# A larger booked cost for the matmuls in a kernel's own list scheduler

## The chip, the core and the metric

The kernel runs on one core of a Trainium2 chip. The metric is the device time of one execution in microseconds (us). The core's engines are called by the profile's names: PE (TensorE, matmuls), DVE (VectorE), ACT (ScalarE), POOL (GpSimd) and SP (which here only issues DMAs). Each engine runs its own instructions strictly in the order in which they were issued, and waits on semaphores for the others.

## What is computed

Causal attention with a cumulative decay (4 batches of 8 heads, 576 positions, head size 64), then a gated feed-forward, then a low-rank mix over the positions with a second feed-forward:

```python
attn = softmax(q @ k.T / 8 + min(-(cum_i - cum_j), 0), causal) @ v   # x: [4, 576, 512]
h    = relu(x @ w_in)                                 # 512 -> 1024
x    = (h * sigmoid(conv3(h))) @ w_out                # 1024 -> 512
u    = x + (x^T @ U @ V)^T                            # rank 32 over the positions
out  = u + relu(u @ w_ch1) @ w_ch2                    # 512 -> 2048 -> 512
```

Everything is float32. The kernel gets this precision by splitting each operand into a high and a low part and using three matmuls where one would do (high by high, high by low, low by high).

## The kernel before

**Stages.** The span falls into stages that overlap: the attention heads and the first feed-forward together (to about 413 us; `m1_in` makes `h`, `m1_out` makes `y`), the mix (`mix_a`, `mix_t`, `mix_b`; T, x and u), then `m2_in` (428 to 629 us) and `m2_out` (629 to 826 us).

`m2_in(f, g)` (L1139 and on) computes one block of the second feed-forward's first product with Strassen's scheme in Winograd's form: seven products, named in program order A11, S2, A12, S3, S1, A22, S4, for each of 8 blocks f of the weights and 4 blocks g of the tokens. One product is six matmuls of 288 columns into one PSUM bank, so a group is 42 matmuls. A bank becomes free when its readers are done. A11, A12 and S4 are read by a copy on ACT (`p1`, `p2`). S2, S3, S1 and A22 are read by additions on DVE at L1169 (`s6`, `s7`, `s5`, `c2`). So `s6_1_1` is the addition that frees the bank of product `ma1_1_S2`.

The operands of `m2_in` are made while it runs. Weights come packed and are decoded by one instruction at L504 and two at L514 on DVE (`wf_w2a3_1` is half 1 of block 3), then added and subtracted at L1115 (`S12`, `S34`). The token blocks T1 to T4 are made by subtractions at L1052. In this text "filler" means these instructions of DVE: nothing on PE waits for them at once, whereas the additions of L1169 hold banks.

**The scheduler.** No instruction is issued where it is written. Each piece of work is recorded as `plan.op(engine, cost, ...)`, with a cost in nanoseconds. `Plan.order()` (L182 on) then simulates the engines with these costs: it takes the engine that is free first, gives it the ready piece that stands first in program order, and books its cost. The order in which the simulated engines took the pieces is the order in which they are issued. So a cost never appears as a wait on the chip, but it decides what stands in front of what, on all engines.

The eight PSUM banks are handed out in the same simulation. Among the banks that are already free at the simulated time, the one freed last is taken:

```python
ready = [i for i in idle if idle[i] <= t]
if ready and used[b.cls] < CAPS[b.cls]:
    o, slot = top[2], min(ready, key=lambda i: -idle[i])
```

So the plan hands a bank on at once if it believes that its reader has just finished. On the chip, the semaphore decides.

**Costs.** `mm(n)` (L347) is the cost of one matmul of n columns. It is used, times the count, for the scores of heads 8 and up (`2*mm`, L675), `m1_in` (`3*mm(290)`, L868), `m1_out` (`3*mm(288)`, L910), `mix_b` (`mm(288)`, L973), `m2_in` (`6*mm(288)`, L1153) and `m2_out` (`3*mm(512)` and `3*mm(256)`, L1252). DVE is booked by L328, which has two fixed parts, 70 ns early and 155 ns late in the program, and 1.042 ns per column (0.52 for the copies and the shift of L504). Scores of heads 0 to 7, transposes and the products with v have costs of their own.

Of the kernel before, what the change touches and what calls it, by code (L numbers as in the profile page):

```python
# [308 lines left out]
def tile_attention_moe_mixer(  # L309
# [35 lines left out]
        return plan.op("PE", ns, fn, r, w)  # L345

    def mm(n, m=128):  # L347
        return max(n / 2.4 + 3, m / 1.2)


    def hi_act(out, src, r, w, n):
# [318 lines left out]
    def products(h, ps, rows, q0, k0, w):  # L670
        d = st[h]

        def mms():
            for c, t in enumerate(d["qk"]):
                nc.tensor.matmul(  # L675
                    ps[:rows, :w],
                    lhsT=t[:, 0, q0 : q0 + rows],
                    rhs=t[:, 1, k0 : k0 + w],
                    start=c == 0,
                    stop=c == len(d["qk"]) - 1,  # L680
                )

        pe(16 + 1.88 * w if h in FS else 2 * mm(w, rows), mms, d["qk"], [ps])
# [173 lines left out]
    def m1_in(b, hf, f):  # L857
        ps = bank("h", f"h{b}_{hf}_{f}")
        c0 = hf * HS
        for kt in range(KT):  # L860
            th, tl = xs[b, kt]

            def mms(kt=kt, th=th, tl=tl):
                a, l = th[:, c0 : c0 + W], tl[:, c0 : c0 + W]
                wh = w1h[f, 0][:, kt * 128 : kt * 128 + 128]
                wl = w1l[f, 0][:, kt * 128 : kt * 128 + 128]
                for n, (ww, xx) in enumerate(((wh, a), (wh, l), (wl, a))):
                    nc.tensor.matmul(  # L868
                        ps[:, :W], lhsT=ww, rhs=xx, start=kt + n == 0, stop=kt == KT - 1 and n == 2
                    )  # L870

            pe(3 * mm(W), mms, [w1h[f, 0], w1l[f, 0], th, tl], [ps])
# [26 lines left out]
    def m1_out(b, hf, dt):  # L899
        if hf == 0:  # L900
            x2[b, dt] = ring(mx, "x2", RINGS["x2"], [128, S], F32, f"x2_{b}_{dt}")
        ps = bank("y", f"y{b}_{hf}_{dt}")
        for f in range(NF1):
            gh, gl = gs[b, hf, f]

            def mms(f=f, gh=gh, gl=gl):
                c0 = dt * 128
                wh, wl = w1h[f, 512][:, c0 : c0 + 128], w1l[f, 512][:, c0 : c0 + 128]
                for n, (ww, xx) in enumerate(((wh, gh), (wh, gl), (wl, gh))):
                    nc.tensor.matmul(  # L910
                        ps[:, :HS], lhsT=ww, rhs=xx(), start=f + n == 0, stop=f == NF1 - 1 and n == 2
                    )

            pe(3 * mm(HS), mms, [w1h[f, 512], w1l[f, 512], gh, gl], [ps])
        o = x2[b, dt]
        act(HS, lambda: nc.scalar.mul(o[:, hf * HS : hf * HS + HS], ps[:, :HS], 2.0**-9), [ps], [(o, hf)])
# [654 lines left out]
```

## Time and profile before

| | |
|---|---|
| time, median of 3 runs | 833.66 us (832.91 to 836.38) |
| the profiled execution's own time | 831.95 us |
| its span, first to last instruction | 830.2 us |
| PE busy | 791.6 us (95%) |
| DVE, ACT, POOL busy | 538.2, 454.3, 360.0 us |
| mean granted clock of PE | 0.996 |

PE is busy for 95% of the span and so idle for 38.6 us. About half of the idle time lies in the first 100 us. The trace has three things to look at: how PE's idle time is spread over the stages, what ended each idle stretch, and what the engine that ended it was doing before. "Idle" behind an instruction is the time for which its engine stood still just before it.

### The profile page before, as it was taken

How to read it: one execution, taken by the hardware profiler on the slowest of the kernel's cores; microseconds unless marked ns; L12 is line 12 of the kernel's file. 1: busy time of each engine (PE TensorE's matmuls, PEld its weight loads, DVE VectorE, ACT ScalarE, POOL GpSimd, SP SyncE). 2: the span in 40 equal slices, each digit the busy share in tenths (PEclk: the TensorE clock that was granted, in tenths of full speed). 3: DMA queues.
4: the chain of work that ended last, by engine and by line, in shares of the span. 5: the costliest groups of instructions: out<-in, count | busy, mean ns of one | idle time of the engine just before them, and what ended most of it. 6: DMA issues, size and time to landing. Idle time of an engine off the chain costs nothing. (4 is left out here: it accounts for less than half of the span.)

```text
span 830.2 us, 15394 instructions
## 1 busy us (share of the span) xinstructions
PE 791.6 (95%) x5300; PEld 709.2 (85%) x5300; DVE 538.2 (65%) x1182; ACT 454.3 (55%) x1144; POOL 360.0 (43%) x441
## 2 busy tenths in 40 slices
PE   4898899999999999999989999999999999999998
PEld 2566788999899999999988898999998888888888
DVE  6887797636855378556998989777688632323232
ACT  4897898858878488767656334324344322222212
POOL 4786684634537234383284776455564200000000
PEclk9999999999999999999999999999999999999999
DMA  7657755734466247030235335446378563636443
GB/s 212 184 170 192 167 154 149 167 97 107 142 144 156 60 111 208 5 109 1 85 109 181 126 133 191 162 150 191 123 220 301 154 193 100 189 103 184 114 127 98
DMA packets 66310, 119.70 MB, mean 144 GB/s; under 512 B 9396, under 2 KB 34868, under 8 KB 66232
## 3 DMA queue, kind: packets, MB, share of 16 engines
q1 hardware_dynamic: 66160, 118.70, 49.7%
q8 instruction: 42, 0.69, 0.4%
q14 instruction: 36, 0.29, 0.1%
q10 hardware_dynamic: 72, 0.01, 0.0%
HBM read 68.81 MB, written 28.90 MB: 118 GB/s over the span
## 5 line engine op out<-in xcount | busy, mean ns | idle before, releaser
L1252 PE MATMUL my<-mh,w 128*128 128x512 f32 (+1 forms) x560 | 158.8, 368 | 0.0
L1153 PE MATMUL ma_S<-u,W 128*128 128x288 f32 x768 | 120.5, 298 | 5.0 <-DVE s L1169 5.0
L1233 DVE SCALAR_TENSOR_TENSOR ml<-ml,mh 128x512 fp32r<-128x512 f32 (+1 forms) x80 | 53.1, 672 | 105.2 <-ACT mh L1230 105.0
L1230 ACT ACTIVATE mh<-ml 128x512 fp32r<-128x512 f32 (+1 forms) x80 | 46.9, 589 | 128.3 <-DMA ml<-ch_d 76.9
L1252 PEld LDWEIGHTS my<-mh,w 128*128 128x128 f32 x560 | 101.7, 189 | 17.5
L910 PE MATMUL y<-gh,w1o 128*128 128x288 f32 x512 | 114.2, 301 | 1.1 <-POOL w1o L364 1.0
L1153 PEld LDWEIGHTS ma_S<-u,W 128*128 128x128 f32 x768 | 108.3, 189 | 7.2 <-DVE s L1169 7.1
L664 POOL TENSOR_SCALAR P<-P,sm 128x128 f32<-128x128 f32 (+3 forms) x128 | 77.1, 618 | 80.3 <-DVE sm L727 63.2
L1252 PE MATMUL my<-ml,w 128*128 128x512 f32 (+1 forms) x280 | 103.0, 368 | 0.0
L1153 PE MATMUL ma_A<-u,W 128*128 128x288 f32 x576 | 92.5, 295 | 0.9 <-ACT p L1165 0.9
L636 DVE CUSTOM_DVE_ANT_0 sc<-sc,mask 128x128 f32<-128x128 f32 (+2 forms) x144 | 68.6, 498 | 34.5 <-PE sc L675 32.5
L910 PEld LDWEIGHTS y<-gh,w1o 128*128 128x128 f32 x512 | 85.0, 188 | 2.2 <-POOL w1o L364 1.3
L364 POOL TENSOR_TENSOR gl<-c,gh 128x288 fp32r<-128x288 f32 x64 | 53.5, 841 | 74.7 <-ACT gh L895 64.4
L868 PE MATMUL h<-xh,w1h 128*128 128x290 f32 x256 | 80.9, 316 | 3.0 <-ACT P L653 0.9
L1153 PEld LDWEIGHTS ma_A<-u,W 128*128 128x128 f32 x576 | 82.0, 188 | 1.6 <-ACT p L1165 1.1
L880 DVE SCALAR_TENSOR_TENSOR c<-h,cw,c 128x288 f32<-128x288 f32 x128 | 64.4, 512 | 26.9 <-ACT c L876 25.8
L868 PE MATMUL h<-xl,w1h 128*128 128x290 f32 x256 | 76.9, 300 | 0.2 <-POOL xl L364 0.2
L868 PE MATMUL h<-xh,w1l 128*128 128x290 f32 x256 | 76.5, 299 | 0.0
L910 PE MATMUL y<-gl,w1o 128*128 128x288 f32 x256 | 74.8, 292 | 0.0
L653 ACT ACTIVATE P<-sc,sm 128x128 f32<-128x128 f32 (+3 forms) x128 | 67.7, 532 | 10.6 <-DVE sm L636 9.2
L352 ACT COPY th<-pt 128x384 f32<-128x384 f32 (+2 forms) x128 | 63.1, 493 | 8.7 <-PE pt L798 7.7
L798 PE MATMUL pt<-ident,P 128*128 128x128 f32 x320 | 59.9, 275 | 1.4 <-ACT th L352 0.8
(139 smaller groups left out, 1734.4 us busy)
## 6 DMA issues: line engine op xcount, KB each, us to landing
ml<-ch_d SPq DMA_DIRECT2D x64, 256.0 KB, 2.8
ch_d<-p SPq DMA_DIRECT2D x64, 144.0 KB, 1.8
raw_w<-w_in SPq DMA_DIRECT2D x16, 512.0 KB, 4.5
raw_w2a<-w_in SPq DMA_DIRECT2D x16, 512.0 KB, 4.8
raw_w2b<-w_in SPq DMA_DIRECT2D x16, 512.0 KB, 4.3
t<-qk_in SPq DMA_DIRECT2D x24, 288.0 KB, 3.1
qkB<-t SPq DMA_DIRECT2D x24, 288.0 KB, 3.8
qkA<-t SPq DMA_DIRECT2D x24, 288.0 KB, 3.9
```

Source lines behind the costliest of these rows:

```text
L352: act(n, lambda: nc.scalar.copy(out(), src()), r, w)
L364: pool(n, lambda: nc.gpsimd.tensor_tensor(out(), src(), f32(hi()), ALU.subtract), r, w, two=True)
L636: lambda: nc.vector.tensor_tensor_reduce(out=ps[:rows, :w], in0=ps[:rows, :w], in1=mask[:rows, m0 : m0 + w], scale=-0.125, scalar=3.0e38 i ...
L653: lambda: nc.scalar.activation(out(), ps[:rows, :w], ACTF.Exp, bias=low(), scale=-1.0, accum_out=total()),
L664: lambda: nc.gpsimd.tensor_scalar(t[:, :w], t[:, :w], r(), 1.0, ALU.mult, ALU.mult),
L798: nc.tensor.transpose(pt[:, o + rows - 128 : o + rows], d["P"][i][:, 128 * j : 128 * j + 128], turn)
L868: nc.tensor.matmul(ps[:, :W], lhsT=ww, rhs=xx, start=kt + n == 0, stop=kt == KT - 1 and n == 2)
L880: lambda k=k: nc.vector.scalar_tensor_tensor(c(), hh[:, k : k + HS], cw[:, 3 * f + k : 3 * f + k + 1], c(), ALU.mult, ALU.add),
L910: nc.tensor.matmul(ps[:, :HS], lhsT=ww, rhs=xx(), start=f + n == 0, stop=f == NF1 - 1 and n == 2)
L1153: nc.tensor.matmul(ps[:, :HS], lhsT=ww, rhs=uu, start=k == 0, stop=k == 5)
L1233: lambda: nc.vector.scalar_tensor_tensor(ml[:, :n], raw(), 0.0, f32(mh[:, :n]), ALU.max, ALU.subtract),
L1252: nc.tensor.matmul(ys[c][dt][:, :n], lhsT=ww, rhs=xx[:, :n], start=f + k == 0, stop=f == NF2 - 1 and k == 2)
```

## The change

One line: the cost that the scheduler books for a matmul.

```diff
     def mm(n, m=128):
-        return max(n / 2.4 + 3, m / 1.2)
+        return max(n / 2.4 + 13.3, 110 if m == 128 else 57)
```

A matmul of 288 columns is booked at 133.3 ns instead of 123, one of 512 at 226.6 instead of 216.3, one of 256 at 120 instead of 109.7. The second term is a floor by the number m of weight columns: 106.7 becomes 110 ns for m = 128 (which decides for matmuls of 128 columns), and 53.3 becomes 57 ns for m = 64. No instruction is added or removed by the code. The order of all engines and the banks change with it: PE's order is the same up to about 70 us and again from 456 us on, with exchanges of a few neighbouring groups between, while DVE, ACT and the banks differ in most stretches.

**At about 97 us on ACT** (head 9, `th9_3` is the copy that head 9's last product with v reads; `gh0_0_4` reads a result of DVE). Before:

```order
L352 COPY th9_2_1250<-pt9_2_1217 128x384
L653 ACTIVATE p4_1_150,sm4_1_342<-sc10_4_0_1185,sm4_1_342 128x288
L895 CAST gh0_0_4_1266<-c0_0_4_1201 128x288
L352 COPY th9_3_1272<-pt9_3_1254 128x320
L653 ACTIVATE p4_1_150,sm4_1_342<-sc10_4_1_1192,sm4_1_342 128x288
```

After the change:

```order
L352 COPY th9_2_1240<-pt9_2_1221 128x384
L895 CAST gh0_0_3_1246<-c0_0_3_1175 128x288
L886 ACTIVATE c0_0_4_1201<-c0_0_4_1201 128x288
L352 COPY th9_3_1262<-pt9_3_1242 128x320
L653 ACTIVATE p4_1_150,sm4_1_342<-sc10_4_0_1187,sm4_1_342 128x288
L653 ACTIVATE p4_1_150,sm4_1_342<-sc10_4_1_1197,sm4_1_342 128x288
L895 CAST gh0_0_4_1286<-c0_0_4_1201 128x288
```

`gh0_0_4` and the second part of `p4_1` have moved from in front of `th9_3` to behind it, as has the first part of `p4_1`.

**At about 418 us on DVE** (`c3_1_7` is the last gate of the first feed-forward, `wf_w2a2_0` a weight decode for block 2 of `m2_in`, `S34_1` a weight sum). Before:

```order
L889 SCALAR_TENSOR_TENSOR c3_1_6_5656<-c3_1_6_5656,h3_1_6_5580 128x288
L1115 TENSOR_TENSOR S34_1_5713<-wf_w2a1_0_5513,S12_1_5684 128x256
L880 SCALAR_TENSOR_TENSOR c3_1_7_5715<-h3_1_7_5634,cw_819,c3_1_7_5715 128x288 x2
L1052 TENSOR_TENSOR T1_1_5749<-u1_5667 128x576
L889 SCALAR_TENSOR_TENSOR c3_1_7_5715<-c3_1_7_5715,h3_1_7_5634 128x288
```

After the change:

```order
L1115 TENSOR_TENSOR S34_1_5668<-wf_w2a1_0_5515,S12_1_5663 128x256
L504 TENSOR_SCALAR wf_w2a2_0_5713<-raw_w2a2_5578 128x512
L514 SCALAR_TENSOR_TENSOR wf_w2a2_0_5713<-raw_w2a2_5578,wf_w2a2_0_5713 128x512 x2
L880 SCALAR_TENSOR_TENSOR c3_1_7_5730<-h3_1_7_5647,cw_819,c3_1_7_5730 128x288 x2
L1052 TENSOR_TENSOR T1_1_5758<-u1_5681 128x576
L889 SCALAR_TENSOR_TENSOR c3_1_7_5730<-c3_1_7_5730,h3_1_7_5647 128x288
```

The three decode instructions of `wf_w2a2_0` now stand in front of the gate `c3_1_7`; before, they came some instructions behind it.

**At about 461 to 468 us in `m2_in`**, PE and DVE. The products S1, A22 and S4 of group (1, 1) on PE, with the engine on which the first matmul of each waits for its bank or operand. Before:

```order
L1153 MATMUL ma1_1_S1_6264<-u1_5667,W1_5695 128x288 [waits Activation_49]
L1153 MATMUL ma1_1_S1_6264<-u1_5667,W1_5695 128x288 x5
L1153 MATMUL ma1_1_A22_6276<-u1_5667,W1_5695 128x288 [waits Activation_49]
L1153 MATMUL ma1_1_A22_6276<-u1_5667,W1_5695 128x288 x5
L1153 MATMUL ma1_1_S4_6287<-u1_5667,W1_5695 128x288 [waits DVE_49]
L1153 MATMUL ma1_1_S4_6287<-u1_5667,W1_5695 128x288 x5
```

After the change:

```order
L1153 MATMUL ma1_1_S1_6272<-u1_5681,W1_5675 128x288 [waits DVE_49]
L1153 MATMUL ma1_1_S1_6272<-u1_5681,W1_5675 128x288 x5
L1153 MATMUL ma1_1_A22_6283<-u1_5681,W1_5675 128x288 [waits Activation_49]
L1153 MATMUL ma1_1_A22_6283<-u1_5681,W1_5675 128x288 x5
L1153 MATMUL ma1_1_S4_6291<-u1_5681,W1_5675 128x288 x6
```

S1 now waits on DVE, for the bank that `s6_1_1` frees, and S4 for nothing; before, S4 had that bank. A few instructions later on DVE (`T1_3` is a filler, the names s and c are additions that free banks), before:

```order
L1169 TENSOR_TENSOR c2_1_1_6339<-ma1_1_S1_6264,s7_1_1_6324 128x288
L1169 TENSOR_TENSOR s6_2_0_6341<-ma2_0_S2_6306,p1_2_0_6315 128x288
L1169 TENSOR_TENSOR s7_1_1_6324<-ma1_1_A22_6276,s7_1_1_6324 128x288
L1169 TENSOR_TENSOR s7_2_0_6360<-ma2_0_S3_6330,s6_2_0_6341 128x288
L1169 TENSOR_TENSOR s5_2_0_6363<-ma2_0_S1_6343,s6_2_0_6341 128x288
```

After the change:

```order
L1169 TENSOR_TENSOR c2_1_1_6322<-ma1_1_S1_6272,s7_1_1_6308 128x288
L1052 TENSOR_TENSOR T1_3_6326<-x2_3_0_5536,u3_5910 128x288
L1169 TENSOR_TENSOR s7_1_1_6308<-ma1_1_A22_6283,s7_1_1_6308 128x288
L1169 TENSOR_TENSOR s6_2_0_6338<-ma2_0_S2_6314,p1_2_0_6324 128x288
L1052 TENSOR_TENSOR T1_3_6326<-x2_3_1_5608,u3_5910 128x288
L514 SCALAR_TENSOR_TENSOR wf_w2a3_1_6063<-raw_w2a11_5938,wf_w2a3_1_6063 128x512
L1169 TENSOR_TENSOR s7_2_0_6361<-ma2_0_S3_6340,s6_2_0_6338 128x288
```

Two halves of `T1_3` and one decode now stand in front of `s7_2_0`, which frees the bank of `ma2_0_S3`.

## Rows read from the trace of the kernel before

**Rows 1.** Windows of the span; columns: length, busy of each engine, clock, DMA.

```profile
core 0: us, PE busy (x) PEld busy (x) DVE busy (x) ACT busy (x) POOL busy (x), PEclk, DMA share, GB/s
0.00:100.00 100.00, 78.97 (x497) 55.90 (x499) 77.79 (x212) 75.08 (x212) 62.79 (x94) 0.98 0.70 187
100.00:400.00 300.00, 296.63 (x2245) 271.57 (x2242) 192.36 (x528) 225.85 (x619) 148.53 (x214) 1.00 0.45 115
400.00:456.00 56.00, 51.38 (x371) 49.82 (x370) 49.83 (x80) 35.52 (x80) 32.35 (x28) 0.97 0.38 124
456.00:487.00 31.00, 28.58 (x209) 27.66 (x208) 30.66 (x51) 10.95 (x23) 23.28 (x21) 1.00 0.39 134
487.00:575.00 88.00, 84.61 (x625) 83.19 (x624) 71.14 (x125) 34.08 (x79) 52.07 (x50) 1.00 0.52 167
575.00:640.00 65.00, 64.84 (x454) 62.75 (x453) 48.95 (x86) 26.84 (x56) 35.29 (x32) 1.00 0.65 205
640.00:830.20 190.20, 186.61 (x914) 158.35 (x912) 67.44 (x105) 45.99 (x79) 5.69 (x4) 1.00 0.48 144
```

**Rows 2.** Timeline of PE (start us, us, instruction): products of `m2_out`, then of `m2_in`.

```profile
699.83 0.61 PE L1252 MATMUL my<-mh,w 128*128 128x512 f32 x2
700.51 0.61 PE L1252 MATMUL my<-mh,w 128*128 128x512 f32 x2
...
560.05 0.96 PE L1153 MATMUL ma_S<-u,W 128*128 128x288 f32 x6
560.85 0.43 PE L1153 MATMUL ma_A<-u,W 128*128 128x288 f32 x2
```

**Rows 3.** Timeline of PE, then of ACT; in brackets the idle time before and its releaser.

```profile
81.27 0.30 PE L798 MATMUL pt<-ident,p 128*128 128x128 f32 x1 [1.83 <-ACT P L653]
...
83.32 0.47 PE L798 MATMUL pt<-ident,p 128*128 128x128 f32 x1 [0.46 <-ACT P L653]
...
99.64 0.49 PE L824 MATMUL av<-th,vr 128*64 128x320 f32 x2 [1.10 <-ACT th L352]
...
98.83 0.43 ACT L895 CAST gh<-c 128x288 fp32r<-128x288 f32 x1 [1.70 <-DVE c L889]
99.17 0.42 ACT L352 COPY th<-pt 128x320 f32<-128x320 f32 x1
```

**Rows 4.** Windows after two pairs of waits; the third column from the right is the clock.

```profile
83.40:86.90 3.50, 3.50 (x16) 3.48 (x17) 1.28 (x4) 2.61 (x8) 3.02 (x5) 0.52 1.02 208
438.30:441.80 3.50, 3.50 (x14) 2.67 (x13) 3.05 (x6) 2.49 (x5) 2.67 (x3) 0.51 0.71 256
```

**Rows 5.** Line L514 on DVE, 400 to 500 us: ns minimum/median/maximum.

```profile
L514 DVE SCALAR_TENSOR_TENSOR wf_w2a<-raw_w2a,wf_w2a x15: 677/936/1886, 404.6 to 499.0; 128x512 int32<-128x512 int32 x15
```

**Rows 6.** Timeline of PE, then of DVE, around 431 to 438 us.

```profile
433.26 0.33 PE L927 MATMUL tp<-ident,x 128*128 128x128 f32 x1 [2.02 <-ACT x L916]
...
437.75 0.41 PE L946 MATMUL t<-xth,uhl 128*64 128x512 f32 x1 [2.60 <-DVE s L1169]
...
431.51 4.32 DVE L514 SCALAR_TENSOR_TENSOR wf_w2a<-raw_w2a,wf_w2a 128x512 int32<-128x512 int32 x3
```

**Rows 7.** Timeline of DVE, then of PE, around 459 to 478 us.

```profile
459.89 1.69 DVE L1052 TENSOR_TENSOR T<-x,x 128x288 f32<-128x288 f32 x1
464.08 0.45 DVE L1169 TENSOR_TENSOR s<-ma_S,p 128x288 f32<-128x288 f32 x1
...
460.53 1.76 PE L1153 MATMUL ma_S<-u,W 128*128 128x288 f32 x12
462.13 0.96 PE L1153 MATMUL ma_A<-u,W 128*128 128x288 f32 x6
464.58 1.07 PE L1153 MATMUL ma_S<-u,W 128*128 128x288 f32 x6 [1.49 <-DVE s L1169]
...
477.70 0.40 PE L1153 MATMUL ma_A<-u,W 128*128 128x288 f32 x1 [0.86 <-ACT p L1165]
```

**Rows 8.** Waits of PE over the whole span: us in total, times, longest.

```profile
PE ma_S L1153 <- DVE s L1169: 5.0, 8, 1.5
```

## The prediction

> **What bounds the kernel now.** The windows of the span come first [rows 1]. PE is the bound: length less PE's busy time gives its idle time by stretch, namely 21.0 us up to 100, 3.4 from 100 to 400, 4.6 from 400 to 456, 2.4 from 456 to 487, 3.4 from 487 to 575, 0.2 from 575 to 640 and 3.6 behind that. The change adds and removes no matmul, so it can only move this idle time and the spells of low clock. The same rows show who is near PE: from 456 to 487 us DVE is busy for 30.66 of 31 us. There anything more on DVE ahead of what PE wants is paid by PE. From 487 to 575 DVE has 16.9 us to spare and makes PE wait only in bursts, and from 640 on it is no bound at all.
>
> Next comes the spacing of equal matmuls [rows 2]. Three products of 512 columns start 0.68 us apart, so 227 ns each; six of 288 columns take 0.80 us, so 133 ns each. The booking after the change says 226.6 and 133.3, the one before 216.3 and 123. So the plan's PE was about 10 ns per matmul too fast, and will be right.
>
> Then what DVE really takes. A decode at L514 lasts 0.68 us at best, 0.94 in the middle and 1.89 at worst [rows 5]; the plan books (155 + 512 x 1.042) ns = 0.69 us, its best case. Three in a row took 4.32 us, 1.44 each [rows 6]. A subtraction at L1052 that the plan books at 155 + 288 x 1.042 = 455 ns took 1.69 us [rows 7]. In the plan of before, PE and DVE were both booked too short, and partly these errors cancelled. After the change only DVE is. The plan then believes DVE to have more room per group of products than it has, and fills it.
>
> **The change part by part.** The sum is made against the profiled execution, 831.95 us, which is 1.71 us below the median.
>
> *Up to 100 us.* On ACT, `gh0_0_4` waits 1.70 us for DVE and stands in front of `th9_3`, for which PE then waits 1.10 us at 99.64 [rows 3]. After the change it stands behind. Also gone is the reason for PE's 0.46 us at 83.32, because the bank is another one. That removes 1.56 us. Against it, other score and transpose groups get a bank that was freed only just before in the plan; I take 0.5 us for two such, by the nearest row, 0.46 us. Net -1.0 us. The bounds are all three waits of PE in these rows gone (-3.4) and the two removed coming back with one more of 1.5 us behind them (+1.5).
>
> *The low clock.* Behind the pair of waits at 81.27 and 83.32 the granted clock is 0.52 for 3.5 us [rows 3, 4], about the lower of the engine's two levels (1.2 of 2.4 GHz), and the same is seen at 438.3 after the waits of 2.02 and 2.60 us [rows 4, 6]. A single wait of 1.49 us at 464.58 was not followed by it. Each spell costs 3.5 x 0.48 = 1.7 us. Since one wait of the first pair goes, I give half of one spell back: -0.8 us (-1.7 to 0).
>
> *100 to 400 us.* PE's idle time is 3.4 us in 300 and the exchanges are of neighbours. A few h and t1 groups get a bank with a shorter lead. I take one more wait of the size of the 0.46 us row: +0.5 us (-1 to +4; the upper end is four waits of 1.1 us).
>
> *400 to 456 us.* Three decodes now stand in front of the gate `c3_1_7`: one at L504 and two at L514, 0.7 + 2 x 0.94 = 2.6 us (median of L514 [rows 5], and for L504 its shortest). PE's last `m1_out` product waits for that gate. But PE then waits 2.02 and 2.60 us anyway [rows 6], and those waits end when DVE is through with a row of work that holds the same decodes. What is paid earlier is saved later, so a quarter stays: +0.7 us (-0.5 to +2.5).
>
> *456 to 487 us.* Before, S4 of group (1, 1) waited for the bank that `s6_1_1` frees. That addition ends at 464.08 + 0.45 = 464.53, and S4 starts at 464.58, where it could have started at 462.93 (0.80 us after A22 at 462.13); 1.65 us are lost [rows 7]. After the change S1, two products earlier, has this bank. It could start at 460.53 + 0.80 = 461.33 and would start at 464.58: 3.25 us lost, 1.60 more. Then `s7_2_0` gets a decode more ahead, 0.94 us, in a stretch where DVE has 0.3 us to spare; the two halves of `T1_3` stood in the same stretch before. Of the 0.86 us that PE waits for ACT at 477.70, a later PE saves about half, 0.4. Net +2.1 us. The lower bound is -1 (the wait at 477.70 goes and the addition comes 1.6 us sooner), the upper +5 (twice the 2.5 us that are added).
>
> *487 to 575 us.* PE waits for DVE's additions eight times, 5.0 us in all [rows 8]; without the 1.49 us of above, seven times and 3.5 us. After the change a decode or a weight sum more stands ahead of seven of the bank-freeing additions here, at some 0.94 us each, 6.6 us. DVE has 16.9 us to spare and takes most of it up between the bursts; a fifth gives +1.3 us (0 to +3).
>
> *575 to 640 us.* The same happens up to the last groups, by one to three fillers, but PE is idle for 0.2 us there, so the leads are long: +0.4 us (0 to +2). *From 640 us on* PE's order is unchanged, and it was full: 0.
>
> Sum: -1.0 - 0.8 + 0.5 + 0.7 + 2.1 + 1.3 + 0.4 = +3.2 us, so 835.2 for an execution like the profiled one and **836.9 us** against the median.
>
> A rule speaks against the change. Six products of 288 columns took 0.80 us [rows 2]. The Trainium skill, in "TensorE: Matmul & The Clock Gate", section "Back-to-back issue gap", gives an isolated gap of N / 2.4 + 2.5 ns, which is 122.5 ns for 288 columns, and less in a sustained stream. By this the old booking would be right and the new one 10.8 ns too long. A group of 42 matmuls would be booked 0.45 us too long, and the 21 groups between 456 and 575 us could be given 9.5 us of fillers for which there is no time; by the page the sum would rise by up to that (an estimate). The trace disagrees, with 133 ns, so this gets no chance of its own.
>
> **The rivals.** *A, the correct booking pays (faster).* With PE right in the plan, a bank that is handed on is really free, and the operands come in the order in which PE needs them. Then the waits of 0.46, 1.10, 1.49 and 0.86 us go [rows 3, 7], 3.9 us together, with one spell of low clock (1.7) and a tenth of the seven other waits (0.4): 833.66 - 6.0 = 827.7 us. For it: the new numbers are those of the rows. Against it: it is ACT and DVE that end these waits, and their booking stays.
>
> *B, the full price of the fillers (slower).* The place is 456 to 575 us. Nothing is taken up by room on DVE: 2.5 us in the saturated stretch, 2.0 before it at `c3_1_7`, two fifths of 6.6 us (2.6) in the bursts, 0.8 behind them. The longer wait of 3.25 us and a second one close behind it bring a spell of low clock, as at 83.4 and 438.3 (1.7). With -1.0 early and +0.5 after that, the sum is 9.1: 842.8 us. It decides if two waits of PE of over half a us come as close together there as the two at 81.27 and 83.32. For it: DVE's 30.66 of 31 us. Against it: a wait ahead shortens the one behind.
>
> *C, nothing moves.* The sequence of products from 456 us on is the same, and the waits only change their names: 833.66, within 1 us.
>
> **How the numbers follow.** About 0.5% (4.2 us) is what a measurement of this kernel can tell from no change, so the bounds lie at 829.5 and 837.8 us. My forecast has a chance of 0.41, of which 0.29 stay below 837.8 and 0.12 do not, since its own range is 833 to 840. A has 0.20, B 0.24 and C 0.15. Faster by over 0.5% is A: 0.20. Within it is 0.29 + 0.15 = 0.44. Slower is 0.12 + 0.24 = 0.36. The range for 8 in 10 takes in the forecast and C, and reaches into A and B until about a tenth is left out on either side: 828.5 to 843.0 us.
>
> **What would show it.** If I am right, PE's matmul time is the same and all of the difference is idle time and spells of low clock; the wait before the `av` at about 99 us is gone; in group (1, 1) of `m2_in` the S1 product waits for 2 to 3.5 us, and S4 does not; PE's idle time from 456 to 487 us grows from 2.4 to 4 or 5 us with DVE still full; and behind 640 us nothing changes. I would be wrong if DVE is through with its row before 456 us sooner than before, because then the additions come early enough and the S1 wait shrinks; or if the spells of low clock move, since each is worth half of my sum.

## The result, and the profile after

The changed kernel takes **842.65 us** (median of 4 runs, 842.38 to 843.54) against 835.02 us for four runs of the kernel before. These medians lie 7.6 us apart. The ratio on record, which is not the quotient of the two medians, is 1.0113 with an interval of 1.0084 to 1.0142, or 9.4 us. So the change costs about 1%. The forecast was slower too, but by 3.2 us; the time is that of rival B (842.8). The profiled execution has a span of 840.3 us, 10.1 us longer than before.

The windows of the changed kernel, cut as in [rows 1] (columns as there):

```profile
core 0: us, PE busy (x) PEld busy (x) DVE busy (x) ACT busy (x) POOL busy (x), PEclk, DMA share, GB/s
0.00:100.00 100.00, 81.25 (x510) 56.69 (x511) 78.73 (x218) 76.70 (x215) 64.81 (x96) 0.98 0.68 188
100.00:400.00 300.00, 292.00 (x2201) 266.01 (x2200) 188.28 (x519) 221.89 (x611) 144.55 (x213) 1.00 0.44 113
400.00:456.00 56.00, 52.08 (x384) 50.52 (x384) 50.14 (x84) 36.23 (x81) 32.18 (x27) 1.00 0.39 129
456.00:487.00 31.00, 27.83 (x202) 26.71 (x201) 30.43 (x52) 11.34 (x24) 24.05 (x21) 1.00 0.41 138
487.00:575.00 88.00, 85.28 (x614) 81.77 (x612) 64.14 (x116) 32.96 (x76) 55.15 (x50) 1.00 0.50 159
575.00:640.00 65.00, 60.72 (x441) 59.13 (x442) 47.92 (x89) 23.98 (x52) 34.91 (x32) 1.00 0.57 175
640.00:840.30 200.30, 196.80 (x959) 166.75 (x957) 72.99 (x111) 50.29 (x87) 8.77 (x7) 1.00 0.49 151
```

PE's idle time is length less busy time. Up to 100 us it fell from 21.0 to 18.8 us. From 100 to 400 us it rose from 3.4 to 8.0, and from 575 to 640 us from 0.2 to 4.3. From 456 to 487 us it rose from 2.4 to 3.2. The windows are cut at fixed times, though, and the work slides through them. The start of the same instruction in both traces is exact. Take the first product, A11, of the second group of `m2_in`, (0, 1), and of its last group, (7, 3). In the timeline of PE (start, duration, instruction), first before, then after:

```profile
445.88 0.30 PE L1153 MATMUL ma_A<-u,W 128*128 128x288 f32 x1
...
623.29 0.30 PE L1153 MATMUL ma_A<-u,W 128*128 128x288 f32 x1
```

```profile
447.92 0.29 PE L1153 MATMUL ma_A<-u,W 128*128 128x288 f32 x1
...
633.05 0.29 PE L1153 MATMUL ma_A<-u,W 128*128 128x288 f32 x1
```

The stretch between them, called **the late stretch** from here on, took 177.4 us before and 185.1 us after: 7.7 of the 10.1 us. The start of other instructions, read in the same way, gives the rest: the two traces are level at the first scores of head 16 (156.71 and 156.64 us), the changed kernel is 3.8 us behind at the start of the last product of `m1_in` (412.02 and 415.85), and 2.0 us behind at group (0, 1).

Idle time alone does not account for this. PE's recorded busy time grew too, from 791.6 to 796.0 us over the span. These are the windows of the late stretch, before and after (columns as above):

```profile
445.88:623.29 177.41, 171.59 (x1270) 169.26 (x1269) 144.28 (x257) 68.87 (x154) 105.03 (x100) 1.00 0.51 164
447.92:633.05 185.13, 175.53 (x1271) 169.65 (x1269) 143.87 (x257) 69.22 (x155) 112.33 (x101) 1.00 0.50 160
```

The idle time rose from 5.8 to 9.6 us, and the busy time by 3.9 us, with the same products and a granted clock of 1.00 in both. A product that has waited is itself recorded longer, as here in the changed kernel (S3, S1 and A22 of group (4, 2); in brackets the idle time before and its releaser):

```profile
555.87 0.96 PE L1153 MATMUL ma_S<-u,W 128*128 128x288 f32 x6
557.78 1.06 PE L1153 MATMUL ma_S<-u,W 128*128 128x288 f32 x6 [0.95 <-ACT p L1165]
558.68 0.96 PE L1153 MATMUL ma_A<-u,W 128*128 128x288 f32 x6
```

S1 starts 1.91 us behind S3 instead of 0.80, and A22 starts 0.90 us behind S1 instead of 0.80. So a wait of 0.95 us of idle time cost 1.2 us. In the late stretch 10 products started late before the change and 24 after it. Take every matmul there that starts more than 0.19 us behind the one ahead, and count the time above the usual 0.13 us: it adds up to 8.4 us before and 16.1 after. The difference is the whole of the 7.7 us.

These are some of the larger waits of PE after the change (timeline of PE):

```profile
176.93 0.40 PE L868 MATMUL h<-xh,w1h 128*128 128x290 f32 x1 [1.50 <-DVE c L889]
...
242.42 0.49 PE L824 MATMUL av<-th,vr 128*64 128x320 f32 x2 [1.35 <-ACT th L352]
...
465.21 0.40 PE L1153 MATMUL ma_S<-u,W 128*128 128x288 f32 x1 [1.50 <-DVE s L1169]
...
575.65 0.40 PE L1153 MATMUL ma_S<-u,W 128*128 128x288 f32 x1 [0.84 <-DVE s L1169]
...
611.73 0.40 PE L1153 MATMUL ma_S<-u,W 128*128 128x288 f32 x1 [1.36 <-ACT p L1165]
...
631.34 0.40 PE L1153 MATMUL ma_A<-u,W 128*128 128x288 f32 x1 [1.11 <-ACT p L1165]
```

The products of `m1_in` and `m2_in` among them wait for the reader of the bank's previous owner: `c1_0_0` at 176.93, `s6_1_1` at 465.21 as forecast, `s6_5_1` at 575.65, and a copy `p2` at 557.78 (shown above), 611.73 and 631.34. The av product at 242.42 waits for a copy of transposed scores that is its own operand as well as the reader in its bank, so this wait can't be put down to the bank. Behind 480 us the waits for copies are new. The timeline of ACT, and of PE just before, around 611 us:

```profile
610.74 0.65 ACT L501 ACTIVATE raw_w2b<-raw_w2b 128x512 f32<-128x512 f32 x1 [2.33 <-DMA raw_w2b<-w_in]
611.30 0.38 ACT L1165 COPY p<-ma_A 128x288 f32<-128x288 f32 x1
...
608.61 0.96 PE L1153 MATMUL ma_A<-u,W 128*128 128x288 f32 x6
609.41 0.96 PE L1153 MATMUL ma_S<-u,W 128*128 128x288 f32 x6
```

On ACT the multiply of the raw weights (L501) stood in front of the copy, and it waited 2.33 us for a weight load. Then came the copy `p2_5_3` of product A12 (608.61). Product S1, two products later, had been given A12's bank by the plan and had to wait for the copy. ACT had also waited for loads in this stretch before, while no product of PE wanted the bank so soon. This is the longest such wait, in the trace of the kernel before; PE is not idle anywhere from 573 to 623 us there:

```profile
578.45 0.68 ACT L501 ACTIVATE raw_w2b<-raw_w2b 128x512 f32<-128x512 f32 x1 [2.57 <-DMA raw_w2b<-w_in]
```

The spells of low clock behind [rows 4] are gone. The windows of the changed kernel (the clock third from the right):

```profile
20.00:25.00 5.00, 4.84 (x20) 3.55 (x20) 4.43 (x10) 2.73 (x9) 4.00 (x6) 0.66 0.48 152
83.40:86.90 3.50, 2.39 (x18) 2.00 (x16) 0.85 (x4) 3.50 (x11) 1.85 (x4) 1.00 1.05 209
436.00:442.00 6.00, 3.13 (x23) 2.45 (x22) 5.93 (x7) 4.51 (x10) 5.96 (x5) 1.00 0.83 283
```

At 83.4 and at 436 us the granted clock is 1.00. There is one spell in the first 25 us, where both kernels have the same order and the one before had none. It is not what makes the changed kernel 1.0 us late at 65 us, ahead of the first place where the orders differ: the same transpose starts at 19.19 us before and 20.16 after, 0.97 us late ahead of the spell, and another behind it at 24.59 and 25.57, 0.98 us late. PE was slower in the spell, but in the trace of before it waited 0.69 and 0.78 us for copies there, and these waits are gone.

### The profile page after: what moved, and what is told of

Its sections match the earlier page's. It is cut to its first block, busy times and chain, and to the rows that moved or that the text cites. A ratio compares the mean times of both kernels' runs of the same rounds, so it can differ in the third digit from the quotient of the medians.

```text
span 840.3 us, 15405 instructions
## 1 busy us (share of the span) xinstructions
PE 796.0 (95%) x5300; PEld 707.6 (84%) x5300; DVE 532.6 (63%) x1182; ACT 453.4 (54%) x1144; POOL 364.4 (43%) x441
```

## The experiments

"Before" is the kernel before, timed beside the kernel of the row: 835.02 us for the first row, 832.1 to 832.8 for the others. Kernels of different groups of runs are better compared by their ratios than by their times. "Late" is the late stretch of the one profiled execution; in `after_longest_free`, `before_longest_free`, `m2in_only`, `before_filler` and `before_all` it holds a spell of 3.4 us at half the clock, worth 1.7 us, and in the others none.

| kernel | median us | ratio to before (interval) | late us |
|---|---|---|---|
| changed kernel | 842.65 | 1.0113 (1.0084 to 1.0142) | 185.1 |
| after_longest_free | 827.87 | 0.9946 (0.9920 to 0.9971) | 174.0 |
| before_longest_free | 826.92 | 0.9921 (0.9890 to 0.9953) | 174.0 |
| m2in_only | 841.93 | 1.0104 (1.0076 to 1.0132) | 186.5 |
| all_but_m2in | 837.69 | 1.0059 (1.0036 to 1.0081) | 178.6 |
| m2in_fix6 | 832.65 | 1.0004 (0.9985 to 1.0023) | 178.8 |
| m2in_fix7 | 834.02 | 1.0031 (1.0010 to 1.0052) | 180.8 |
| floor_only | 831.30 | 0.9988 (0.9967 to 1.0010) | 177.7 |
| after_act212 | 843.61 | 1.0132 (1.0107 to 1.0157) | 182.8 |
| after_rest1000 | 833.78 | 1.0008 (0.9987 to 1.0029) | 179.4 |
| after_filler | 824.96 | 0.9903 (0.9885 to 0.9920) | 170.9 |
| after_load | 839.77 | 1.0092 (1.0065 to 1.0118) | 181.6 |
| all_fifo | 820.41 | 0.9850 (0.9836 to 0.9865) | 169.0 |
| before_filler | 822.38 | 0.9874 (0.9831 to 0.9916) | 174.4 |
| before_all | 826.60 | 0.9938 (0.9918 to 0.9958) | 175.7 |
| filler_fifo | 820.04 | 0.9854 (0.9803 to 0.9905) | 170.1 |

### Is it the banks or the order?

One edit to the choice of the bank, in the changed kernel and in the one before:

```diff
-    o, slot = top[2], min(ready, key=lambda i: -idle[i])
+    o, slot = top[2], min(ready, key=lambda i: idle[i])
```

Expected of the changed kernel with it:

> The changed kernel with one more edit: among the free PSUM banks the plan takes the one that has been free longest, instead of the one freed last. The order of every engine is word for word that of the changed kernel; 627 of 708 products get another bank. Theory H (hand-on): the lost time is PE waiting in banks that the plan hands on at once while their reader on DVE or ACT is late on the chip. By the trace these waits sum to about 20 us behind 100 us, and most should vanish: 822 to 832 us, with no wait over 0.5 us on line 1153 behind 480 us. Theory O (order): the lost time is what stands in front of PE's operands (decoded weights, T blocks, gates), whichever bank is used: 840 to 845 us, as without the edit.

And of the kernel before with it:

> The kernel before with the same edit of the bank choice and the same order of every engine as before. Theory H: its own bank waits (about 14 us behind 50 us) go too: 822 to 830 us, and the distance to the changed kernel with this edit shrinks from 9 us to under 3. Theory O: 832 to 836 us, and the distance stays near 9.

Measured: 827.87 and 826.92 us. By the ratios the edit takes 1.7% (about 14 us) off the changed kernel and 0.8% (about 7 us) off the one before, and the two then differ by 1 us. The late stretch is 174.0 us in both. What is left of waits on line 1153 in the changed kernel with the edit (waits of PE: total, times, longest):

```profile
PE ma_S L1153 <- ACT p L1165: 2.5, 1, 2.5
PE ma_A L1153 <- DVE s L1169: 0.4, 1, 0.4
```

The three longest rows of line 1153 in the changed kernel without it are:

```profile
PE ma_S L1153 <- DVE s L1169: 3.6, 7, 1.5
PE ma_S L1153 <- ACT p L1165: 2.8, 3, 1.4
PE ma_A L1153 <- ACT p L1165: 2.3, 2, 1.2
```

The wait of 2.5 us stands at 478 us; behind 480 us there is none over 0.4 us. So theory H holds: with the orders of all engines unchanged, the late loss is there or not by the choice of the bank alone. The different order of DVE's fillers costs PE nothing in the late stretch if the bank isn't handed on at once. The times understate what the edit saves in waits: the four runs of the changed kernel have a mean granted clock of 0.997 to 0.998, and the seven with the edit 0.987 to 0.993. The time lost by this, the span times one less the clock, is some 2 us in the first and 6 to 11 us in the second (an estimate).

### Which booking does it?

The new cost for `m2_in` alone, and for everything else:

```diff
# m2in_only
-            pe(6 * mm(HS), mms, keys, [ps])
+            pe(6 * max(HS / 2.4 + 13.3, 110), mms, keys, [ps])
# all_but_m2in (in the changed kernel)
-            pe(6 * mm(HS), mms, keys, [ps])
+            pe(6 * (HS / 2.4 + 3), mms, keys, [ps])
```

> The kernel before, with the new cost only for the products of m2_in (line 1153, 6 x 133.3 ns); all other matmuls are booked as before. By the places where the two traces part, the changed kernel loses 3.8 us between 157 and 390 us, gains 1.8 in the mix, and loses 1.0 from 456 to 487, 2.2 from 487 to 575 and 4.4 from 600 to 630. If the loss belongs to the late stage's own booking, this kernel shows about +7 us, all behind 446 us: 839 to 843. If it is a matter of which order a plan happens to fall into, the late losses appear at other places and with another sum: anything from 830 to 845, and the single waits of the changed kernel (S1 of group 5_3, A22 of group 7_2) don't recur.

> The changed kernel, with the old cost for the products of m2_in alone. If the late stage's booking makes the loss, the early part is that of the changed kernel (+3.8 us at 390, +2 at 446) and the rest that of before: 835 to 838 us. If it depends on the order that a plan happens to fall into: 830 to 845, with late waits of its own.

Measured: 841.93 us, with a late stretch of 186.5, and 837.69 with 178.6. The timeline of PE in `m2in_only` has the waits of the changed kernel at the same products: S1 of (1, 1), S1 of (5, 3) and A22 of (7, 2).

```profile
462.01 0.40 PE L1153 MATMUL ma_S<-u,W 128*128 128x288 f32 x1 [2.16 <-DVE s L1169]
...
609.72 0.40 PE L1153 MATMUL ma_S<-u,W 128*128 128x288 f32 x1 [1.42 <-ACT p L1165]
...
629.05 0.40 PE L1153 MATMUL ma_A<-u,W 128*128 128x288 f32 x1 [0.84 <-ACT p L1165]
```

So the late loss belongs to the booking of `m2_in` and comes back with it. The other matmuls' booking costs 5.1 us by the medians (837.69 against 832.57), of which 1.2 lie in the late stretch. Its trace is 4.6 us behind at group (0, 1), but it also has longer spells of low clock up to there, so the place of the rest is not shown. The two parts cost 9.4 and 5.1 us by the medians, more together than the whole change.

The floor alone:

```diff
-        return max(n / 2.4 + 3, m / 1.2)
+        return max(n / 2.4 + 3, 110 if m == 128 else 57)
```

> The kernel before with the new floor by the number of weight columns alone (110 and 57 ns), the fixed part at 3 ns. It touches scores of 128 columns or 64 rows; 19 places on PE differ from before and 307 products get another bank, none of them at a distance of two products. Both theories: the late stage is that of before, 831 to 836 us; only a few waits of the attention part move.

Measured: 831.30 us, late 177.7. The floor is of no account; the fixed part does it.

### A threshold in the plan?

In the plan of before no bank of `m2_in` came back after a distance of two products; in the changed one, 63 of 212 do. A distance of two means that only one product lies in between, which was booked at 738 and is now booked at 800 ns, while a copy on ACT frees its bank in 756 ns by the plan's numbers. Three runs tested whether passing this mark is the cause:

```diff
# m2in_fix6 and m2in_fix7, in the kernel before (6 or 7)
-            pe(6 * mm(HS), mms, keys, [ps])
+            pe(6 * (HS / 2.4 + 6), mms, keys, [ps])
# after_act212, in the changed kernel
-    "ACT": (162, 142, 175, 159, 200),
+    "ACT": (212, 142, 175, 159, 200),
```

> The kernel before, with the fixed part of the products of m2_in alone raised from 3 to 6 ns (6 x 126 ns a product). Theory T (threshold): in the plan a copy on ACT frees a bank 197 + 397 + 162 = 756 ns after its product ends; a product booked at 6 x 126 = 756.0 ns is just too short for the bank to be taken again after one product in between, so no bank comes back at a distance of two products (0 of 210 in the plan, as before). The waits of S1 in group 5_3 and A22 in group 7_2 stay away: 831 to 836 us, and the stretch from the first product of group 0_1 to that of group 7_3 as long as before (177.4 us) within 2 us. Theory F (fillers): the loss grows with the booked length, so 3 of 10.3 ns bring a third of it: 835 to 837 us and 179.5 to 180.5 us.

> The same with 7 ns (6 x 127 ns): one nanosecond per matmul more than the run beside it. 762 ns are over 756, so 54 banks come back at a distance of two products in the plan; the orders differ in 6 places on PE, 33 on DVE and 16 on ACT. Theory T: the loss is there nearly whole, 838 to 842 us, the stretch from group 0_1 to 7_3 at 182 to 187 us, with waits of over 0.9 us of S1 or A22 for an ACT copy. Theory F: within 1 us of the run with 6 ns.

> The changed kernel with the booked hand-over from ACT to PE at 212 instead of 162 ns. The copy then frees its bank 806 ns after the product, over the 800 ns that a product is booked, and no bank comes back at a distance of two products, though PE stays booked at its true length. Theory T: the waits behind ACT copies in the late stage (557, 611, 631 us) go, and from group 0_1 to 7_3 it takes 177 to 181 us instead of 185.1; with the early loss kept, 835 to 839 us. Theory F: 841 to 845, since the fillers stand as in the changed kernel.

Measured: 832.65, 834.02 and 843.61 us; late 178.8, 180.8 and 182.8. Theory T fell: it was met at 6 ns, but 7 ns gave 834.02 us and not 838 to 842, late 180.8 and not 182 to 187. Theory F's price for the first 3 ns (835 to 837 us, late 179.5 to 180.5) wasn't there either. The step from 6 to 7 ns costs 1.9 us of the late stretch, the 3 ns below it 1.4, and the way from 7 to 13.3 (`m2in_only` without its spell) another 4.1; these are differences of single traces. With the hand-over booked longer, the waits behind ACT copies shrink from 5.1 to 2.3 us, but those behind DVE grow from 3.6 to 6.8, as the waits of PE show (to be compared with those of the changed kernel above):

```profile
PE ma_S L1153 <- DVE s L1169: 6.8, 9, 1.6
PE ma_A L1153 <- ACT p L1165: 2.3, 3, 1.2
```

There S1 gets the bank of S2, which stands three products ahead, and waits 0.8 to 1.0 us for `s6` in five groups behind (1, 1). Closing one distance only moves PE to the next late reader. By the last product of `m1_in` this run is also 10 us behind the kernel before, and it changes other banks up to there; most of it lies in spells of low clock (0.69 from 80 to 90 us, 0.66 from 110 to 120, 0.88 and 0.95 from 240 to 260: some 8 us). So its time, though it lies in the range of theory F, says nothing about the late stage.

A version that keeps the order, but lets a bank rest:

```diff
+    rested = [i for i in ready if idle[i] + 1000 <= t]
-    o, slot = top[2], min(ready, key=lambda i: -idle[i])
+    o, slot = top[2], max(rested or ready, key=lambda i: idle[i] if rested else -idle[i])
```

> The changed kernel, where the plan still takes the bank freed last, but only among those that have been free for 1 us or more in the plan (if there is none, the one free longest). The order of every engine is word for word that of the changed kernel; no bank comes back before a distance of four products, most at exactly four. Theory H: readers that are late by less than about 1.8 us no longer reach PE. The waits of 0.3 to 1.5 us on line 1153 behind 480 us (8.8 us in the trace) go, and from the first product of group 0_1 to that of 7_3 it takes 174 to 177 us instead of 185.1: 828 to 834 us. If it is not distance but something else in the choice of the longest-free bank that helped: 838 us or more.

Measured: 833.78 us, late 179.4. By the ratios it takes 1.05% back, about 9 us, so distance does count, but the readers are sometimes later than such a rest: the late stretch is 2 us above what was expected, with waits of 0.95 and 0.93 us of A22 for `s6` in groups (2, 3) and (3, 1).

### Why are the readers late?

Two candidates: DVE's fillers, booked too short (the step of the prediction), and the copies that stand behind a multiply waiting for its load.

```diff
# after_filler: dve(..., more), added to the cost in the late stages
     L504 decode, shift        more=400
     L514 decode               more=270
     L1052 T blocks            more=450
     L1115 S12, S34            more=380
# after_load: late loads of raw_w2a and raw_w2b
-                late = wire + 980 - end
+                late = wire + 980 - end + o.lag      # 3000 for these, else 0
```

> The changed kernel, with the fillers of the late stages on DVE booked at about the mean that the traces show (decodes +270 and +400 ns, subtractions of T +450, sums of weights +380), the bank choice as it is. Theory P (the step of the prediction): PE waits because the plan believes that DVE has room for fillers ahead of the additions; booked truly, the waits on DVE behind 456 us (6.1 us) mostly go: 836 to 839 us, 179 to 182 us from group 0_1 to 7_3. Theory L (late copies): the larger part of the late loss is PE waiting for copies on ACT that stand behind a multiply of raw weights whose load has not landed, and DVE's booking doesn't touch it: 840 to 843 us, at least 183 us.

> The changed kernel, with the landing of the late weight loads (w2a, w2b) booked 3 us later, so that the multiply of the raw weights on ACT is not put in front of a copy while its data is on the way. Theory L: the waits for copies at 533, 557, 611, 631 and 634 us (5.3 us) go: 836 to 839 us, 179 to 182 us from group 0_1 to 7_3. Theory P: 841 to 844 us, since DVE's fillers stand as they are.

Measured: 824.96 us with the fillers booked truly, late 170.9; 839.77 us with the loads booked later, late 181.6. The first is faster than the kernel before by 0.8 to 1.2%, though it still hands banks on at once: 58 of 210 at a distance of two. Its windows from 456 us to the end of `m2_in`, and then all that is left of PE's waits in `mix_b` and `m2_in` (lines 973 and 1153 in the changed kernel, 977 and 1159 here):

```profile
456.00:487.00 31.00, 30.79 (x230) 30.32 (x229) 28.12 (x49) 11.01 (x24) 23.46 (x20) 1.00 0.35 119
487.00:575.00 88.00, 88.00 (x661) 87.75 (x660) 69.00 (x135) 36.26 (x82) 53.62 (x52) 1.00 0.60 187
575.00:624.00 49.00, 49.00 (x359) 48.28 (x359) 37.83 (x69) 19.55 (x42) 29.48 (x27) 1.00 0.59 182
```

```profile
PE mh L977 <- DVE s L1175: 0.7, 1, 0.7
PE ma_A L1159 <- DVE s L1175: 0.2, 1, 0.2
```

PE is full, and the waits behind ACT copies are gone as well, which theory P had not asked for. So the fillers' short booking is a cause, and the larger one: 14.2 us of the late stretch. The edit changes orders and banks too, so it shows what the booking is worth, not through which of the waits. It isn't the whole: `after_load` took 3.5 us off the late stretch, as theory L had it (179 to 182 us), and its waits behind `p2` copies at 557, 611 and 631 us are gone.

### Does the new matmul cost help or harm by itself?

The kernel before, with true fillers; all three edits with the new and with the old cost; and the fillers with the longest-free bank, loads as they were:

> The kernel before (old cost of the matmuls) with DVE's late fillers booked at about the mean of the traces, as in the run of the changed kernel at 825 us. With both runs there is a square: matmul cost old or new, fillers short or true. Theory C (two errors that cancelled): PE booked too short and DVE too short fitted each other; with DVE true and PE 10 ns a matmul too short, the plan gives fillers too little room and brings operands too late: 833 to 842 us, over 8 us slower than with the new matmul cost. Theory D (DVE alone): the fillers' booking is all that matters: 823 to 828 us, and the new matmul cost is worth nothing by itself.

> The changed kernel with all three edits: the longest-free bank, DVE's fillers at their mean, late loads booked 3 us later. If banks are all of it, the other two add nothing to the longest-free bank: 825 to 830 us. If fillers and loads cost PE by its operands too: 820 to 825.

> The kernel before with the longest-free bank, true fillers and late loads 3 us later, but the old cost of the matmuls: the counterpart of the run at 820.4 us. Theory C: 828 to 836 us. Theory D: 819 to 823 us.

> The changed kernel with true fillers and the longest-free bank, loads as they were. If the loads' booking was of no account in the run at 820.4 us: 820 to 823 us; if the copies behind late loads still mattered: 824 to 827.

Measured: 822.38, 820.41, 826.60 and 820.04 us. With true fillers and the old bank choice, the old matmul cost is 2.6 us better than the new, which is not clear of noise (the intervals of the two ratios overlap); with the longest-free bank and the late loads, the new one is 6.2 us better, which is (`all_fifo` and `before_all` differ in nothing else). In the late stretch the new cost is ahead in both pairs, 170.9 against 174.4 and 169.0 against 175.7 us, of which 1.7 are a spell in each run with the old cost. Theory C (two errors that cancelled) falls with the first of these: with the old matmul cost and true fillers the kernel isn't slower, but 10 us faster than before. Theory D falls with the second. `before_filler` has one wait of 2.8 us for `s6_1_1` in the late stretch, `before_all` the same one with 4 us, and the products of `m2_in` in the two runs with the new cost wait 0.4 us at most. The waits of PE on `m2_in`'s line (1159 there) in `before_filler`:

```profile
PE ma_A L1159 <- DVE s L1175: 2.8, 1, 2.8
PE ma_S L1159 <- ACT p L1171: 0.5, 1, 0.5
```

The loads' booking was of no account once the fillers were true and the bank the longest-free (820.41 and 820.04). The best version, 820.04 us, has the new matmul cost, true fillers and the longest-free bank; it beats the kernel before by 1.0 to 2.0%. Its interval overlaps that of `before_filler`, so it is not shown to be better than true fillers alone.

## Why the prediction was right or wrong

**Right.** The sign; that the wait before the `av` product at 99 us goes; that S1 of (1, 1) waits instead of S4, for `s6_1_1`. That wait was 1.50 us instead of 2 to 3.5, since the bank came free sooner: the waiting product started 5.05 us behind the first one of its group (460.16 to 465.21) instead of 6.45 (458.13 to 464.58). PE's idle time from 456 to 487 us grew to 3.2 us and not to 4 or 5, with DVE still full (30.43 of 31 us). The fillers' short booking does turn the new matmul cost into a loss of the late stretch: with short fillers it went from 177.4 to 185.1 us, with true ones from 174.4 (`before_filler`) to 170.9 (`after_filler`). Behind 640 us nothing changed.

**Half right: "all of the difference is idle time and spells of low clock".** Away from waits the matmuls keep their spacing of 133 ns, but of the 10.1 us of span 5.7 are idle time and 4.4 recorded busy time, since a product that has waited is itself recorded longer. The terms of the sum were priced in idle time, and each wait costs about a quarter of a us more. From (0, 3) to (6, 0) the idle time is 3.40 us before and 3.38 after, and the stretch got 2.2 us longer.

**The sum, term by term** (same instruction in both traces; forecast, then measured):

| | forecast | measured |
|---|---|---|
| up to 157 us, with the clock | -1.8 | -0.1 |
| 157 to 412 us | +0.5 | +3.9 |
| 412 us to group (0, 1) | +0.7 | -1.8 |
| (0, 1) to (0, 3), 446 to 484 us | +2.1 | +1.0 |
| (0, 3) to (6, 0), 484 to 573 us | +1.3 | +2.2 |
| (6, 0) to (7, 3), 573 to 623 us | +0.4 | +4.5 |
| behind | 0 | +0.3 |

**Wrong: the last stretch.** The step that failed is "PE is idle for 0.2 us there, so the leads are long". The term of +0.4 us measured +4.5. The idle time of before tells the leads of the banks of before. The change gave out other banks: S1 got that of A12, which stands only two products ahead. In the trace of before ACT stood still for loads in this stretch too (2.57 us at 578.45); a list of the waits of ACT for DMA would have shown a late reader there, whom nobody waited for yet. The prediction had fillers on DVE only in mind. With the same order and the longest-free bank the loss was gone (late 174.0 us), and so it was with true fillers (170.9).

**Wrong: 100 to 400 us.** The term of 0.5 us was mis-sized in the same way, and measured 3.9: two products of `m1_in` got banks whose reader on DVE was late and waited 1.50 and 1.05 us, and an av product waited 1.35. From head 16 to the end of `m1_in` it took 255.3 us before and 259.2 after; with the same order and the longest-free bank it took 254.0 (160.3 to 414.3). So this loss too is one of banks.

**The sizes in the middle**, from (0, 1) to (6, 0), are within their bounds. The mix got 1.8 us shorter where +0.7 was forecast: the spell of low clock at 438 us went, worth 1.7 us, and the two waits of 2.02 and 2.60 us became 1.15 and 1.72, while a new one of 1.06 us came at 429.93. The end of the prediction had named a spell that moves as a sign of being wrong. Both spells of low clock went; the prediction gave half of one back. They are worth 3.4 us, so with them the loss would have been larger. Up to 157 us the waits of 0.46 and 1.10 us went as forecast, but the changed kernel was 0.97 us late by 20 us already, in a part with the same order, and new waits of 1.28 and 0.98 us came at 106 and 109 us.

**Rival B** has the time by luck, not the place. Of its 9.1 us it put 8.8 into 400 to 575 us, with a spell of low clock; from 412 to 573 us 1.4 were measured, with no spell, and most of the loss lies in the 3.9 us ahead and the 4.5 behind. **Rival A** said that a right cost pays. `before_all` and `all_fifo` show that it does (6.2 us) once no bank is handed on at once, the fillers are booked truly and the late loads later; with the longest-free bank alone it doesn't (827.87 against 826.92 us).

## What to carry to other kernels

Correcting one cost of a planner that has other wrong costs is a change of the plan, not of its truth: here a right matmul cost lost 1.1%, right costs of another engine gained 1.3%, and both together with a third edit gained 1.5%, which the intervals do not set apart from 1.3%. A plan that hands on the resource freed last has no slack for a reader that is late; taking the one that has been free longest was worth 0.8% by itself (in `before_all`, beside true fillers, later loads and the old matmul cost, it didn't help: 826.6 against 822.4 us). To forecast such a change, list for each product who freed its bank and how long before, in the new plan, and then see in the old trace how late those readers can be, whoever they are. Price a wait by the start of the same instruction, not by the idle time alone.

## What was not expected

- DVE's instructions in the late stages have no one duration: L514 on 128 x 512 elements takes 0.68 to 1.89 us [rows 5]. The trace of before shows when: of the 64 instructions at L514 that decode the weights of the second feed-forward, the 18 with no instruction of POOL (GpSimd) beside them all took 0.68 to 0.69 us, and every longer one ran beside POOL for a part of its time. The 160 additions at L1169, which have one operand in PSUM, took 0.44 to 0.46 us with POOL beside them or not. One decode instruction ran at 429.91 us in a pause of POOL, and the three of [rows 6], 4.32 us from 431.51 on, ran beside it (timeline of DVE, then of POOL):

```profile
429.91 0.68 DVE L514 SCALAR_TENSOR_TENSOR wf_w2a<-raw_w2a,wf_w2a 128x512 int32<-128x512 int32 x1
...
431.67 1.78 POOL L364 TENSOR_TENSOR u<-u 128x576 fp32r<-128x576 f32 x1 [2.30 <-DVE T L1052]
433.42 1.86 POOL L364 TENSOR_TENSOR u<-T,u 128x576 fp32r<-128x576 f32 x1
435.24 1.72 POOL L364 TENSOR_TENSOR W<-wf_w2a,W 128x512 fp32r<-128x512 f32 x1
```

  The Trainium skill says in "SBUF — State Buffer", section "Who interferes with whom", that DVE and GpSimd share a pair of ports which one instruction holds to its end. The trace fits that; no run here changed what POOL does, so the cause is not shown.
- With the orders of all engines the same, the choice among eight banks moved the time by about 14 us (ratios of 1.0113 and 0.9946).
- Spells of low clock came at other places in executions with the same order (20 to 25 us in the changed kernel, which had none there before). Over a whole execution the mean granted clock went from 1.000 (`after_filler`) to 0.986 (`after_act212`). What decides that stays open.
- `after_load` has the order and banks of the changed kernel up to about 320 us, and its profiled execution was still 5.5 us behind it at 306 us: 2.0 up to 65 us, and most of the rest near two spells of low clock (0.83 from 85 to 95 us and 0.84 from 240 to 250). A single execution of this kernel can be off by such an amount, so that differences of 2 us between single terms say little.
